# Attention with a gated feed-forward factor: the output projection by Strassen's method, and the row sums of the query projection moved

## The chip, the cores and the metric

The kernel runs on one NeuronCore of a Trainium2 chip, as one program with the engines TensorE (PE, matmuls into PSUM), VectorE (DVE), ScalarE (ACT), GpSimd (POOL) and SyncE (SP, which issues the DMAs here). The metric is the device time of one execution in microseconds. Each engine works through its own instructions in order; semaphores tie the engines together.

## What is computed

`x` has 2048 rows of 512 (BF16). There are 32 heads of width 128 with cached keys and values of 2048 rows each. With `xn = layernorm(x)`:

```python
q = (xn @ wq).reshape(heads)                     # 512 -> 32 x 128
p = softmax(q @ k_cache.T * Dh**-0.5)            # per head, 2048 x 2048
s = concat(p @ v_cache) @ wo                     # 4096 -> 512, the output projection
gate = xn @ W_gate; up = xn @ W_up               # 512 -> 1792
g = silu((relu(gate) * up) @ W_down)             # 1792 -> 512
out = x + s * g
```

## The kernel before

It is written engine by engine with explicit semaphores. It has two stages.

**Feed-forward stage** (`emit_gate_up`, `emit_down`). For each of four quarters `Q` of the rows and each of 14 chunks `fc` of the inner width, four 512-wide matmuls make the gate product, four the up product; ScalarE takes the relu, VectorE multiplies. After the 14 chunks `emit_down` makes `g_sb`. The layer norm (`ln_task`) runs inside the first quarter, and DMA transposes write `xnT`. After the last `emit_down`, VectorE makes four sums and differences of the quarters of `xnT` in `emit_tx` (tensor `TX`, lines 661 to 672); GpSimd makes the like of a pair of heads' query weights (`emit_sw`, tensor `SW`).

**Attention stage.** A block `b` is one head `h = b // 4` and one quarter `Q = b % 4` of the queries; there are 128 blocks. A block has eight pairs `p` of key tiles. For each pair, TensorE makes two score tiles (`emit_S_tile`, L806), ScalarE takes their exponential (L818), and TensorE multiplies them by the values (`emit_PV_tile`, L915, eight matmuls 129 wide, the last column giving the softmax's sum). The score pairs run three pairs ahead (`LAG`) of the value products; the plan below is keyed by the block and pair of the value products. A block's result stays in the one accumulator `ps_acc`. At the block's end VectorE normalizes it (`emit_norm_block`, L835 and L838) into one of eight `Onorm` buffers, and a DMA transpose on SyncE's queue writes it to `OT_store`. The next block's first value product waits for the normalization.

**PSUM slots.** Score pairs share a ring of three slots (`ring_acquire`, two banks each) with all inserted groups of matmuls (`emit_M`). Acquisition is strictly in turn and waits until the slot's last reader is done: for a score pair its exponential, for an inserted group its last VectorE operation.

**Inserted groups.** A plan (`at(b, p, ...)`) puts groups of other matmuls into the blocks, at pair 0 or 4:
- `emit_qp`: the query projection of the first two heads, plainly.
- `emit_st`: the query projection of a later pair of heads by Strassen's method, seven products in four steps (two, two, two, one product) for each half of the columns, so eight steps per pair of heads in eight blocks, at p=0.
- `emit_oproj_tile` (lines 755 to 778): the output projection of a group `g` of four heads, 16 row tiles of four 512-wide matmuls (L761), each added by VectorE into the FP32 sum `s_acc` (L774). One tile per block, at p=4, or behind `emit_st`'s single-product step in the same slot. The groups 0 to 6 go this way.
- For group 6, `emit_base` multiplies `s_acc` by `g_sb` and adds it into `x_sb` (L786, L789), tile by tile.
- `emit_final_tile` (L949): the last group's tiles in the last blocks and after them; VectorE multiplies by `g_sb` (L957), adds to `x_sb` (L973), and a DMA writes the output (L978).

SyncE's queue carries, in the order of the code, the loads of keys, values, `wq` and `wo`, the transposes and the output; an instruction on it that waits holds those behind it.

Of the kernel before, what the change touches and what calls it, by code (L numbers as in the profile page):

```python
# [5 lines left out]
BF16 = mybir.dt.bfloat16  # L6
# [46 lines left out]
def bass_recurrent_scan__mha_block_cached__glu_gated_reglu__prompt_kernel(  # L53
# [18 lines left out]
    NQ = 512  # L72
# [14 lines left out]
    NON = 8  # L87
    NQT = 12
    WSC = 512.0
    assert H % 4 == 0 and QB == 4 and (G * QB) % NON == 0 and NON % QB == 0  # L90
# [19 lines left out]
    with ExitStack() as es:  # L110
# [17 lines left out]
        x_sb = S_([128, NT, D], BF16, "x_sb")  # L128
# [9 lines left out]
        PT = [S_([128, 2, NQ], BF16, "PT") for _ in range(NPB)]  # L138
        es_b = ExitStack()
# [5 lines left out]
        xn_sb = SB_([128, NT, D], BF16, "xn_sb")  # L145
# [28 lines left out]
        sem_T = newsem()  # L174
        sem_out = newsem(16)
# [40 lines left out]
        for b in range(2):  # L216
            tok_pool = sem_pool.sig(pool.memset(V_sb[b][:, :, Dh:VW], 2.0))
# [82 lines left out]
        def t_toks(g):  # L300
            return [(sem_ob[i], 16 * TPB * (g + 1)) for i in range(NON)]

# [178 lines left out]

        gr_free = [None] * NSLOT
# [32 lines left out]
        def emit_gate_up(Q):  # L515
            qs = slice(Q * NQ, (Q + 1) * NQ)
            h_tok = None
            for fc in range(FC):
# [27 lines left out]
                h_tok = finish_gate_up(Q, fc, s, gtok, gu_tok)  # L546
            return h_tok
# [54 lines left out]
        fin_tmp = [S_([128, D], BF16, "fin_tmp") for _ in range(4)]  # L602
        TX = S_([128, 4, DC // 2, S // 2], F16, "TX")
        SW = [S_([128, 4, DC // 2, Dh], F16, "SW") for _ in range(2)]
        cu = S_([128, NQ], F32, "cu")
# [50 lines left out]
        HS = S // 2  # L656
        HC = DC // 2
        tx_tok = []
        sw_tok = {}

        def emit_tx():
            b11 = xnT[:, 0:HC, 0:HS]
            b12 = xnT[:, 0:HC, HS:S]
            b21 = xnT[:, HC:DC, 0:HS]
            b22 = xnT[:, HC:DC, HS:S]
            _wait_all(dve, [t for Q in range(QB) for t in xt_ready[Q]])
            t1 = sem_T.sig(dve.tensor_tensor(TX[:, 0], b12, b11, ALU.subtract))
            sem_T.sig(dve.tensor_tensor(TX[:, 2], b22, b12, ALU.subtract))  # L668
            _wait(dve, t1)
            t2 = sem_T.sig(dve.tensor_tensor(TX[:, 1], b22, TX[:, 0], ALU.subtract))  # L670
            _wait(dve, t2)
            tx_tok.append(sem_T.sig(dve.tensor_tensor(TX[:, 3], TX[:, 1], b21, ALU.subtract)))

# [24 lines left out]
        def emit_st(pr, c, step, *banks):  # L698
# [33 lines left out]
            if step == 1:  # L732
                if c == 0:
                    _wait(pe, sw_tok[(pr, 1)])
                    _wait(pe, tx_tok[0])
# [19 lines left out]
        def emit_oproj_tile(g, n, bank):  # L755
            if n == 0:
                _wait_all(pe, t_toks(g))
                _wait(pe, wo_tok(g))
            ins = None
            for hh in range(G):  # L760
                ins = pe.matmul(ps_r[:, bank, 0:D], OT_store[g % 2][:, hh, n * 128:(n + 1) * 128],  # L761
                                Wo_sb[g % 2][:, hh, :], start=(hh == 0), stop=(hh == G - 1))
            otok = sem_op.sig(ins)
            if n == NT - 1:
                opg_tok[g] = otok
                if g + 2 < NG:
                    _wait(sp, otok)
                    issue_wo(g + 2)
            _wait(dve, otok)
            if g == 0:  # L770
                atok = sem_opa.sig(dve.tensor_copy(s_acc[:, n, :], ps_r[:, bank, 0:D]))
            else:
                atok = sem_opa.sig(
                    dve.tensor_tensor(s_acc[:, n, :], s_acc[:, n, :], ps_r[:, bank, 0:D], ALU.add)  # L774
                )
            if g == NG - 2:
                emit_base(n, atok)
            return atok
# [3 lines left out]
        def emit_base(n, after_tok):  # L782
            _wait(dve, after_tok)
            if n == 0:
                _wait(dve, glu_done_tok)
# [311 lines left out]
```

## Time and profile before

| | us |
|---|---|
| median of 3 runs (1280.49 to 1281.59) | 1280.52 |
| the profiled execution's own time | 1280.7 |
| its span, first to last instruction | 1279.4 |
| TensorE busy | 1257.1 |
| ScalarE busy | 1011.1 |
| VectorE busy | 458.8 |
| GpSimd busy | 97.5 |

The feed-forward stage ends near 157 us; the attention stage fills the rest. Busy times are unions of the recorded instructions. Matmuls are pipelined, so one matmul's recorded duration is longer than the distance to the next; prices of matmuls are therefore taken from starts, or from runs of many. "L12" is line 12 of the kernel whose profile it is. Square brackets at the end of a timeline row give the idle time ahead of the instruction and what ended it.

### The profile page before, as it was taken

What the parts mean: (1) busy time and instruction counts of PE and PEld (TensorE: products, weight loads), DVE (VectorE), ACT (ScalarE), POOL (GpSimd) and SP (SyncE); (2) the same over time, 40 slices, a digit from 0 to 9 for tenths busy, and PEclk for the clock granted to TensorE, in tenths of its full rate; (3) what the DMA queues carried; (4) which work ended last, traced back from release to release, by engine and by line L of the source; (5) the groups of instructions that cost most, each with busy time, mean ns of one, the idle gap of its engine ahead of it and who ended that gap; (6) DMA issues with size and microseconds to landing.
All of it is one profiled execution on the core that took longest, in us unless ns stands there. A gap on an engine that the chain in (4) does not pass through costs nothing.

```text
span 1279.4 us, 26927 instructions
## 1 busy us (share of the span) xinstructions
PE 1257.1 (98%) x11740; PEld 828.7 (65%) x11965; DVE 458.8 (36%) x807; ACT 1011.1 (79%) x1112; POOL 97.5 (8%) x100
## 2 busy tenths in 40 slices
PE   9999989999999999999999999999999999999998
PEld 5444456666666666666666666666666666666665
DVE  7433342222332332333333333333333333335455
ACT  3322369998888888888888888888888888888985
POOL 2200020100001010101010010101010101000000
PEclk9999989999999999999999999999999999999999
DMA  9700002323322232322132332332231222232212
GB/s 268 153 1 1 1 18 51 59 50 59 50 50 55 67 59 47 59 49 57 35 58 47 75 51 46 59 67 55 50 59 34 59 47 54 51 67 47 50 18 75
DMA packets 233588, 72.14 MB, mean 56 GB/s; under 512 B 211200, under 2 KB 233472, under 8 KB 233472
## 3 DMA queue, kind: packets, MB, share of 16 engines
q1 hardware_dynamic: 232800, 70.02, 27.8%
q8 instruction: 95, 1.56, 0.5%
q10 hardware_dynamic: 672, 0.39, 0.1%
q14 instruction: 21, 0.17, 0.0%
HBM read 32.77 MB, written 2.10 MB: 27 GB/s over the span
## 4 chain that ended last, share of the span: by engine, by line
PE 86%; ACT 12%; issue 1%; DVE 1%; DVEq 0%
PE ps_acc L915 33%; PE ps_r L806 27%; ACT PT L818 12%; PE ps_r L761 7%; PE ps_r L717 6%; PE ps_acc L562 4%; PE ps_r L543 4%; PE ps_r L539 4%; PE ps_r L949 1%; PE ps_r L645 1%; PE ps_r L375 0%; DVE fin_tmp L957 0%; PE ps_r L441 0%; DVE TX L670 0%; DVE TX L668 0%
## 5 line engine op out<-in xcount | busy, mean ns | idle before, releaser
L818 ACT ACTIVATE PT<-ps_r 128x1024 bf16<-128x1024 f32 x1024 | 960.9, 1036 | 155.1 <-PE ps_r L806 145.3
L915 PE MATMUL ps_acc<-V_sb,PT 128*128 128x129 bf16 x8192 | 764.3, 220 | 9.9 <-ACT PT L818 0.9
L915 PEld LDWEIGHTS ps_acc<-V_sb,PT 128*128 128x128 bf16 x8192 | 612.8, 98 | 246.0 <-ACT PT L818 19.7
L806 PE MATMUL ps_r<-QT_sb,KT_sb 128*128 128x512 bf16 x1849 | 672.3, 380 | 6.2 <-DVE QT_sb L722 5.2
L806 PEld LDWEIGHTS ps_r<-QT_sb,KT_sb 128*128 128x128 bf16 x2048 | 191.9, 98 | 6.5 <-DVE QT_sb L722 5.4
L835 DVE RECIPROCAL rz_sb<-ps_acc 128x4 f32<-128x4 f32 x127 | 23.2, 183 | 445.7 <-PE ps_acc L915 445.7
L774 DVE TENSOR_TENSOR s_acc<-s_acc,ps_r 128x512 f32<-128x512 f32 x96 | 66.0, 688 | 214.4 <-PE ps_r L761 211.4
L761 PE MATMUL ps_r<-Wo_sb,OT_store 128*128 128x512 bf16 x442 | 114.2, 379 | 0.5
L681 POOL TENSOR_SCALAR Wq_sb<-Wq_sb 128x1024 bf16<-128x1024 bf16 x15 | 41.6, 2771 | 856.7 <-DMA Wq_sb<-in_A_wq_dram 856.7
L838 DVE TENSOR_TENSOR Onorm<-ps_acc,rz_sb 128x512 bf16<-128x512 f32 x127 | 87.8, 692 | 4.4
L761 PEld LDWEIGHTS ps_r<-Wo_sb,OT_store 128*128 128x128 bf16 x448 | 43.8, 98 | 52.9 <-ACT PT L818 1.1
L498 ACT ACTIVATE gr_sb<-ps_r 128x512 bf16<-128x512 f32 x55 | 32.6, 596 | 51.0 <-PE ps_r L539 50.4
L504 DVE TENSOR_TENSOR hT<-gr_sb,ps_r 128x512 bf16<-128x512 bf16 x55 | 37.8, 687 | 46.8 <-PE ps_r L543 41.7
L717 PE MATMUL ps_r<-TX,SW 128*128 128x512 f16 x180 | 48.6, 379 | 0.5
L562 PE MATMUL ps_acc<-Wd_sb,hT 128*128 128x512 bf16 x219 | 48.7, 379 | 0.3
L543 PE MATMUL ps_r<-xnT,Wu_sb 128*128 128x512 bf16 x165 | 42.8, 379 | 0.2
L722 DVE TENSOR_TENSOR QT_sb<-cu,ps_r 128x512 bf16<-128x512 f32 x60 | 41.3, 688 | 4.3
L539 PE MATMUL ps_r<-xnT,Wg_sb 128*128 128x512 bf16 x165 | 42.6, 379 | 0.2
L722 DVE TENSOR_TENSOR cu<-cu,ps_r 128x512 f32<-128x512 f32 x60 | 41.3, 688 | 0.0
L562 PEld LDWEIGHTS ps_acc<-Wd_sb,hT 128*128 128x128 bf16 x224 | 21.9, 98 | 26.4
L722 DVE TENSOR_TENSOR QT_sb<-cv,ps_r 128x512 bf16<-128x512 f32 x60 | 38.3, 681 | 0.0
L717 PEld LDWEIGHTS ps_r<-TX,SW 128*128 128x128 f16 x180 | 17.6, 98 | 21.3 <-ACT PT L818 1.5
(85 smaller groups left out, 419.7 us busy)
## 6 DMA issues: line engine op xcount, KB each, us to landing
V_sb<-in_A_v_cache_dram SPq DMA_DIRECT2D x32, 512.0 KB, 4.2
Wq_sb<-in_A_wq_dram SPq DMA_DIRECT2D x16, 256.0 KB, 2.9
Wo_sb<-in_A_wo_dram SPq DMA_DIRECT2D x8, 512.0 KB, 3.6
OT_store<-Onorm SPq DMA_TRANSPOSE x127, 2.5
Wd_sb<-in_B_W_down_dram SPq DMA_DIRECT2D x1, 1792.0 KB, 14.1
x_sb<-in_A_x_dram SPq DMA_DIRECT2D x3, 512.0 KB, 8.5
out_dram<-x_sb SPq DMA_DIRECT2D x6, 256.0 KB, 2.1
Wg_sb<-in_B_W_gate_dram SPq DMA_DIRECT2D x1, 640.0 KB, 9.7
```

The costliest lines, as they stand in the source:

```text
L539: ins = pe.matmul(g_ps, Wg_sb[:, c, fs], xT[:, c, xs], start=(c == 0), stop=(c == DC - 1))
L543: ins = pe.matmul(u_ps, Wu_sb[:, c, fs], xT[:, c, xs], start=(c == 0), stop=(c == DC - 1))
L562: ins = pe.matmul(ps_acc[:, jb, 0:D], hT[par][:, fc, j * 128:(j + 1) * 128], Wd_sb[:, fc, :], start=(fc == 0), stop=(fc == FC - 1))
L681: k = sem_sw.sig(pool.tensor_scalar(wflat, wflat, WSC, None, op0=ALU.mult))
L717: ins = pe.matmul(ps_r[:, bank, :], L(i), R(i), start=(i == 0), stop=(i == HC - 1))
L722: return sem_qpe.sig(dve.tensor_tensor(dst, a, ps_r[:, bank, :], op))
L761: ins = pe.matmul(ps_r[:, bank, 0:D], OT_store[g % 2][:, hh, n * 128:(n + 1) * 128], Wo_sb[g % 2][:, hh, :], start=(hh == 0), stop=(hh == ...
L774: dve.tensor_tensor(s_acc[:, n, :], s_acc[:, n, :], ps_r[:, bank, 0:D], ALU.add)
L806: ins = pe.matmul(ps_r[:, 2 * s + tt, :], KT_sb[h % 2][:, t * 128:(t + 1) * 128], QT_sb[qt_slot[(h, Q)]][:], start=True, stop=True)
L818: act.activation(PT[pb][:], ps_r[:, 2 * s:2 * s + 2, :], ACTF.Exp, scale=scale if h < 2 else scale / WSC)
L838: dve.tensor_tensor(Onorm[ob][:], o_ap, rz_sb[:].to_broadcast([128, 4, Dh]), ALU.mult))
L915: ins = pe.matmul(o_ap, PT[pb][:, tt, j * 128:(j + 1) * 128], V_sb[vb][:, t, 0:VW], start=(t == 0 and j % 2 == 0), stop=(t == KT - 1 and j ...
```

## The change

**Output projection.** For the groups 0 to 6, `emit_oproj_tile` gives way to `emit_os`. The 2048 x 512 result of a group and its operands are cut into halves: rows (first and second 1024), inner width (two heads and two heads), columns (256 and 256). Seven products of halves, in the order of four steps (1 and 2; 6 and 5; 3 and 7; 4), are made for two row tiles of each half at a time: a product is four matmuls 256 wide in one bank. Their results are added straight into the four quarters of `s_acc`, which now hold running sums over the groups in Strassen's intermediate form. Only after group 6 two more additions per four row tiles turn them into the result. The operands' sums come from `emit_ox` on VectorE (tensor `OX`, FP16, four operations per half of the columns) and `emit_wx` on GpSimd (tensor `WX`, with `Wo` scaled by 1024 in place). The values' sum column is set so that the normalized output is 1024 times larger; the factors are taken out in `emit_base` and in the final tiles.

**Plan.** In blocks 16 to 121 every block has one step of `emit_os` and, up to block 121, one of `emit_st`, at p=0 and p=4 in separate slots; the two-product one comes first. `emit_st` begins two blocks later (block 2), and the plain projection of head 1 moves to p=0 of blocks 0 and 1. Group 6's last six steps lie two to a block in 122 to 124; block 125 has no group. `emit_ox` runs at pairs 2 and 3 of the first and eighth block of a group; `emit_base` at set places in blocks 116 to 125 through a queue.

**Row sums.** `emit_tx` is cut into eight operations of 1024 elements and called in the third quarter of the feed-forward stage.

**Memory.** `x_sb` is given up after the feed-forward stage; `TX` lies in the former `xn_sb`; x comes back tile by tile into `xr_sb` (16 DMAs) for `emit_base`, which now adds into `s_acc` in FP32. The final addition reads `s_acc` and writes `g_sb`, from which the output goes. `Onorm` has four buffers in place of eight.

The core of the diff:

```diff
-    NON = 8
+    NON = 4
...
+        def emit_tx(k):
+            c, i = divmod(k, 4)
+            lo = slice(c * NQ, (c + 1) * NQ)
+            hi = slice(HS + c * NQ, HS + (c + 1) * NQ)
...
+            if i == 0:
+                t = dve.tensor_tensor(X[0], b12, b11, ALU.subtract)
...
+                if Q == QB - 2 and 2 <= fc < 10:
+                    emit_tx(fc - 2)
...
-            for hh in range(G):
-                ins = pe.matmul(ps_r[:, bank, 0:D], OT_store[g % 2][:, hh, n * 128:(n + 1) * 128],
-                                Wo_sb[g % 2][:, hh, :], start=(hh == 0), stop=(hh == G - 1))
...
+        def emit_wx(g):
+            W, X = Wo_sb[g % 2], WX[g % 2]
...
+            k = sem_wx.sig(pool.tensor_scalar(wflat, wflat, WOSC, None, op0=ALU.mult))
...
+            k = sem_wx.sig(pool.tensor_tensor(X[:, 0], b12, b11, ALU.subtract))
+            sem_wx.sig(pool.tensor_tensor(X[:, 2], b22, b12, ALU.subtract))
...
+            k = sem_wx.sig(pool.tensor_tensor(X[:, 1], b22, X[:, 0], ALU.subtract))
...
+        def emit_ox(g, c, i):
...
+            if i == 0:
+                _wait_all(dve, t_toks(g, c))
+                _wait(dve, os_tok.get("x"))
+                ox_tok["k"] = sem_ox.sig(dve.tensor_tensor(OX[:, 0], a21, a22, ALU.add))
...
+        def emit_os(g, q, step, *banks):
...
+            def prod(k, bank):
+                for j in range(2):
...
+                    for i in range(GH):
+                        ins = pe.matmul(ps_r[:, bank, j * DH:(j + 1) * DH], L(i), R(i),
+                                        start=(i == 0 and j == 0), stop=(i == GH - 1 and j == 1))
+                return sem_op.sig(ins)
...
+            def acc(k, bank, op=ALU.add, first=False):
+                _wait(dve, os_tok.get((q, k)))
+                if first:
+                    t = dve.tensor_copy(names[k], view(bank))
+                else:
+                    t = dve.tensor_tensor(names[k], names[k], view(bank), op)
+                os_tok[(q, k)] = sem_opa.sig(t)
...
+            if step == 0:
...
+                p1 = prod(1, banks[0])
+                p2 = prod(2, banks[1])
+                _wait(dve, p1)
+                acc("11", banks[0], first=f)
+                k1 = acc("21", banks[0], first=f)
+                _wait(dve, p2)
+                return [k1, acc("11", banks[1])]
+            if step == 1:
+                _wait(pe, ox_tok[(g, c)])
...
+            p4 = prod(4, banks[0])
...
+            k1 = acc("21", banks[0], ALU.subtract)
+            k2 = acc("22", banks[0])
             if g == NG - 2:
-                emit_base(n, atok)
...
+                t = sem_opa.sig(dve.tensor_tensor(c22, c22, c21, ALU.add))
...
+                t = sem_opa.sig(dve.tensor_tensor(c12, c12, c22, ALU.add))
...
+        def issue_xr(k):
+            n = base_order[k]
+            if k >= 4:
+                _wait(sp, base_done[base_order[k - 4]])
+            sem_xr[k % 4].sig(sp.dma_start(xr_sb[:, k % 4:k % 4 + 1, :], x_t[:, n:n + 1, :]))
...
-                dve.tensor_tensor(x_sb[:, n, :], x_sb[:, n, :], s_acc[:, n, :], ALU.add)
+                dve.tensor_tensor(s_acc[:, n, :], s_acc[:, n, :], xr_sb[:, k % 4, :], ALU.add))
...
-                dve.tensor_tensor(x_sb[:, n, :], x_sb[:, n, :], fin_tmp[fb][:], ALU.add))
+                dve.tensor_tensor(g_sb[:, n, :], s_acc[:, n, :], fin_tmp[fb], ALU.add))
...
-        at(0, 4, (emit_qp, 1, 1, 0), (emit_qp, 1, 1, 1))
-        at(1, 4, (emit_qp, 1, 1, 2), (emit_qp, 1, 1, 3))
+        at(0, 0, (emit_qp, 1, 1, 0), (emit_qp, 1, 1, 1))
+        at(1, 0, (emit_qp, 1, 1, 2), (emit_qp, 1, 1, 3))
...
+                it = (emit_os, 1 if i % 4 == 3 else 2, g, i // 4, i % 4)
+                if g < NG - 2 or i < 10:
+                    osteps[b0 + i] = it
                 else:
+                    at(b0 + 10 + (i - 10) // 2, 4 * (i % 2), it)
+            for c in range(2):
+                for i in range(4):
+                    side.setdefault((b0 + 7 * c, 2 + i // 2), []).append((emit_ox, g, c, i))
...
+            if 0 < pr < NPR:
+                c, step = r // 4, r % 4
+                q = (emit_st, 1 if step == 3 else 2, pr, c, step)
+                first, second = (o, q) if step == 3 and o else (q, o)
+                at(b, 0, first)
+                if second:
+                    at(b, 4, second)
...
+        base_at = [(LB - 8 + k // 2, 2 + k % 2) for k in range(4)]
+        base_at += [(LB - 4 + k // 2, 2 + k % 2) for k in range(4)]
+        base_at += [(LB - 1 + k // 2, 2 + k % 2) for k in range(4)]
+        base_at += [(LB + 1, 1 + k) for k in range(4)]
...
-        _wait(dve, glu_done_tok)
-        emit_tx()
         emit_sw(1)
+        emit_wx(0)
...
+            if pq == 2 and bq % GB == 8 and 0 < bq // GB < NG - 1:
+                emit_wx(bq // GB)
```

More of the change, by code (lines that the diff above doesn't have):

```diff
@@ L174, in bass_recurrent_scan__mha_block_cached__glu_gated_reglu__prompt_kernel @@
         sem_T = newsem()
+        sem_ox = newsem()
+        sem_xr = [newsem(16) for _ in range(4)]
+        sem_wx = newsem()
         sem_out = newsem(16)
@@ L766, in emit_oproj_tile @@
                 if g + 2 < NG:
-                    _wait(sp, otok)
+                    _wait(sp, p4)
                     issue_wo(g + 2)
[L769 to L775, printed above, removed]
-            if g == NG - 2:
-                emit_base(n, atok)
@@ L1046, in bass_recurrent_scan__mha_block_cached__glu_gated_reglu__prompt_kernel @@
                     emit_sw(pr)
+            if pq == 1 and bq == (NG - 1) * GB:
+                for k in range(4):
+                    issue_xr(k)
+            if pq == 2 and bq % GB == 8 and 0 < bq // GB < NG - 1:
+                emit_wx(bq // GB)
             if items:
@@ L1054, in bass_recurrent_scan__mha_block_cached__glu_gated_reglu__prompt_kernel @@
             emit_PV_tile(gq, 1)
-        assert not plan
+        assert not plan and not side and not base_queue
         emit_M([(emit_final_tile, 1, NT - 8), (emit_final_tile, 1, NT - 7)])
```

214 lines of the change are left out of this document (150 added, 64 removed).

## The prediction

> **What bounds the kernel now.** I read the page's busy shares and chain first, then one steady block in the timeline, then the places where TensorE stood still.
>
> ```profile
> span 1279.4 us, 26927 instructions
> ...
> PE 1257.1 (98%) x11740; PEld 828.7 (65%) x11965; DVE 458.8 (36%) x807; ACT 1011.1 (79%) x1112; POOL 97.5 (8%) x100
> ...
> PE 86%; ACT 12%; issue 1%; DVE 1%; DVEq 0%
> ```
>
> TensorE (PE) is busy 98% and holds 86% of the chain. Busy alone proves little, so here is a block (one head, one quarter of the queries, eight pairs of key tiles), from the timeline: start, duration, engine, line.
>
> ```profile
> 728.88 0.59 PE L806 MATMUL ps_r<-QT_sb,KT_sb 128*128 128x512 bf16 x2
> 729.08 0.18 DVE L835 RECIPROCAL rz_sb<-ps_acc 128x4 f32<-128x4 f32 x1 [2.42 <-PE ps_acc L915]
> 729.30 0.69 DVE L838 TENSOR_TENSOR Onorm<-ps_acc,rz_sb 128x512 bf16<-128x512 f32 x1
> 729.31 0.59 PE L717 MATMUL ps_r<-TX,SW 128*128 128x512 f16 x2
> ...
> 730.55 1.28 DVE L722 TENSOR_TENSOR QT_sb<-cv,ps_r 128x512 bf16<-128x512 f32 x2
> ...
> 731.49 3.77 ACT L818 ACTIVATE PT<-ps_r 128x1024 bf16<-128x1024 f32 x4 [0.63 <-PE ps_r L806]
> ...
> 732.40 0.38 PE L806 MATMUL ps_r<-QT_sb,KT_sb 128*128 128x512 bf16 x1
> 732.62 0.39 PE L915 MATMUL ps_acc<-V_sb,PT 128*128 128x129 bf16 x4
> 732.84 0.38 PE L806 MATMUL ps_r<-QT_sb,KT_sb 128*128 128x512 bf16 x1
> ...
> 733.28 0.59 PE L806 MATMUL ps_r<-QT_sb,KT_sb 128*128 128x512 bf16 x2
> 733.72 1.03 PE L761 MATMUL ps_r<-Wo_sb,OT_store 128*128 128x512 bf16 x4
> ...
> 734.78 0.69 DVE L774 TENSOR_TENSOR s_acc<-s_acc,ps_r 128x512 f32<-128x512 f32 x1 [2.95 <-PE ps_r L761]
> ...
> 737.89 0.18 DVE L835 RECIPROCAL rz_sb<-ps_acc 128x4 f32<-128x4 f32 x1 [2.42 <-PE ps_acc L915]
> ```
>
> A score tile and its four value matmuls take 732.84-732.40 = 0.44 us, so a pair takes 0.885 and a block's eight pairs 7.08. This block lasts 737.89-729.08 = 8.81, which is 7.08 plus the two inserted groups of four 512-wide matmuls at 0.863: TensorE has no gap. ScalarE needs at most 0.94 for the exponentials of a pair (3.77 for four) and sat idle 0.63 before these four. A block is therefore TensorE's work, and what is taken from that work shortens it, down to ScalarE's 8 x 0.94 = 7.5 us.
>
> **The matmuls of the output projection.** Removed: 7 groups x 16 tiles x 4 = 448 matmuls 512 wide. Added: 7 groups x 4 (two row tiles of each half) x 7 products x 4 = 784 matmuls 256 wide, each with its own weight load. The chain of waits gives durations of runs of matmuls:
>
> ```profile
> 0.76 4.00 PE ps_r L375 x18
> ...
> 7.47 0.89 PE ps_r L441 x16
> ...
> 342.33 0.86 PE ps_r L761 x4
> ```
>
> 512 wide: 0.863/4 = 0.2158 us, so 96.7 us go. No warm 256-wide matmul exists here. 128 wide, one load each, is 0.89/16 = 0.0556; on the straight line between the two, 256 costs 0.0556 + (0.2158-0.0556)/3 = 0.109, so 85.5 come: **-11.2**. The bounds: half of the 512 price (0.1079, -12.1), and the only 256-wide row, L375 at the program's start, 4.00/18 = 0.222 (+77.3). Two more views decide between them, the windows of a stall that is treated below and the weight loads of L645 (512 wide) just after it. Columns of the windows: window, length, busy of PE, PEld, DVE, ACT, POOL with counts, granted clock.
>
> ```profile
> 160.60:165.78 5.18, 0.00 (x0) 0.00 (x0) 4.99 (x5) 0.86 (x1) 4.19 (x3) 0.73 0.00 0
> 165.78:167.00 1.22, 1.22 (x6) 0.71 (x7) 0.00 (x0) 0.00 (x0) 0.00 (x0) 0.50 0.00 0
> ...
> 169.00:169.50 0.50, 0.50 (x2) 0.15 (x1) 0.00 (x0) 0.50 (x1) 0.00 (x0) 0.50 0.00 0
> ...
> 170.00:171.00 1.00, 1.00 (x9) 0.53 (x8) 0.71 (x2) 0.00 (x0) 0.00 (x0) 1.00 0.00 0
> ```
> ```profile
> 168.33 0.15 PEld L645 LDWEIGHTS ps_r<-xnT,Wq_sb 128*128 128x128 bf16 x1 [0.28 <-issue]
> ...
> 168.76 0.15 PEld L645 LDWEIGHTS ps_r<-xnT,Wq_sb 128*128 128x128 bf16 x1 [0.28 <-issue]
> ```
>
> The clock there is 0.50, and L645 starts every 168.76-168.33 = 0.43 us, twice 0.2158, as 0.222 is about twice 0.109. So I take 0.109 and hold L375 for a row of the slow clock. [...]
>
> **VectorE's share.** The 16 additions per group become 40 (ten per four row tiles: 3, 2, 3 and 2 over the four steps), and eight differences of 1024 elements (`emit_ox`) come in two lots of four. Prices, from the groups by line:
>
> ```profile
> L774 DVE TENSOR_TENSOR s_acc<-s_acc,ps_r 128x512 f32<-128x512 f32 x96 | 66.0, 688 | 214.4 <-PE ps_r L761 211.4 <-remote 0.4
> ...
> L681 POOL TENSOR_SCALAR Wq_sb<-Wq_sb 128x1024 bf16<-128x1024 bf16 x15 | 41.6, 2771 | 856.7 <-DMA Wq_sb<-in_A_wq_dram 856.7
> ...
> L789 DVE TENSOR_TENSOR x_sb<-x_sb,s_acc 128x512 bf16<-128x512 bf16 x16 | 11.1, 692 | 0.5
> ...
> L689 POOL TENSOR_TENSOR SW<-Wq_sb 128x256 f16<-128x256 bf16 x15 | 11.0, 734 | 108.3 <-DVE g_sb L582 107.1
> ...
> L973 DVE TENSOR_TENSOR x_sb<-x_sb,fin_tmp 128x512 bf16<-128x512 bf16 x16 | 6.6, 416 | 0.0
> ...
> L667 DVE TENSOR_TENSOR TX<-xnT 128x2048 f16<-128x2048 bf16 x1 | 1.2, 1224 | 0.0
> ```
>
> Two additions of which the second reads the first's result, from the timeline, start 0.79 apart:
>
> ```profile
> 721.14 0.69 DVE L722 TENSOR_TENSOR cu<-cu,ps_r 128x512 f32<-128x512 f32 x1
> ...
> 721.93 0.69 DVE L722 TENSOR_TENSOR cv<-cu,ps_r 128x512 f32<-128x512 f32 x1
> ```
>
> 7 x 24 x 0.69 = 116 us, plus 56 x 0.69 = 38 (0.69 lies between 416 ns for 512 and 1224 for 2048): VectorE goes from 459 to some 610 us, under half the span. What matters is when a PSUM slot comes free. There are three; each score pair and each inserted group takes the next, so the third pair after a group waits for the group's last VectorE operation. Count from a block's start (728.88 above). The group at p=0 has its three operations behind the normalization and is done at 731.83, 2.95; the third pair after it starts at 732.40, 3.52. The new group at p=4 starts at 4.83; its first product ends at 5.27 and its first addition runs 0.2 later (734.78 against matmuls that end at 734.58), at 5.47; three at a pitch of 0.62 ((730.55-729.30)/2 for operations that don't read each other) end at 7.4, and their slot is wanted at 3.52+4.40 = 7.92. In the blocks with four differences before it (14 of them) VectorE gets free at 2.95+4x0.67 = 5.6, and the three end at 7.5. Both fit: **0**. If each addition waits for the one before, the pitch is 0.79, the 14 late ones end at 7.9 and cost up to 0.1 each, 1.4 in all; a gain is excluded, since no pair waits now.
>
> **GpSimd** scales Wo (2048 elements, two of L681, 5.5 us) and forms four differences of 512 elements (two of L689 each, 5.9 us) once per group (`emit_wx`), eight blocks (some 70 us) ahead of their use; the query weights' work in its queue comes four blocks before and after: 0. Were it late, step 1 of a group would wait.
>
> **Sums over rows (`emit_tx`) moved into the feed-forward stage.** Today they hold VectorE, then TensorE:
>
> ```profile
> 158.29 1.22 DVE L667 TENSOR_TENSOR TX<-xnT 128x2048 f16<-128x2048 bf16 x1
> ...
> 165.04 0.69 DVE L722 TENSOR_TENSOR QT_sb<-cu,ps_r 128x512 bf16<-128x512 f32 x1
> 165.78 0.61 PE L806 MATMUL ps_r<-QT_sb,KT_sb 128*128 128x512 bf16 x1 [5.19 <-DVE QT_sb L722]
> ```
>
> TensorE stands 5.19 us because the first Strassen group's slot is freed only behind the four sums; then it runs at a clock of 0.50 from 165.78 to about 169.7, as the windows show, which loses half of 3.9, 1.95. Both go: **-7.1** (at the least -5.2, if the clock falls anyway). What is late next: that group now comes two blocks later, some 17 us, when sums and weight differences are long done. In the feed-forward stage two groups of four 512-wide matmuls pass per 1.73 us while VectorE needs one 0.69; a half sum of 0.69 fits into the rest: 0.
>
> **The end.** The plan leaves block 125 without a group. Its first value matmul waits for the normalization, which above ends at 729.99, 1.11 after the block's start; with only one score tile (0.22) to do before it, and 0.2 until one engine sees another's end, TensorE stands about **+1.1** (0 to 1.3). The `emit_base` pairs (two operations of 0.69) lie two to a block in blocks 116-124, and in 125; behind a three-operation group they end at 2.95+4x0.69 = 5.7, as the differences do: 0 (at most 0.2 in each of four blocks). x comes back in 16 loads on SyncE's queue, each waiting for an `emit_base` long before the block's transposes: 0. Last, the final addition now reads the FP32 sum, which costs 692 ns (L789's form) instead of 416. The last of them:
>
> ```profile
> 1268.21 0.69 DVE L957 TENSOR_TENSOR fin_tmp<-ps_r,g_sb 128x512 bf16<-128x512 f32 x1 [0.22 <-PE ps_r L949]
> ...
> 1271.29 0.69 DVE L957 TENSOR_TENSOR fin_tmp<-ps_r,g_sb 128x512 bf16<-128x512 f32 x1 [0.23 <-PE ps_r L949]
> ...
> 1276.13 0.68 DVE L957 TENSOR_TENSOR fin_tmp<-ps_r,g_sb 128x512 bf16<-128x512 f32 x1
> 1276.73 0.75 DVE L973 TENSOR_TENSOR x_sb<-x_sb,fin_tmp 128x512 bf16<-128x512 bf16 x2
> ```
>
> From 1268.21 VectorE is close to saturated: nine additions x 0.28 = 2.5, less part of the 0.23: **+2.3** (1.6 to 2.5). Four Onorm buffers instead of eight: a transpose has four blocks, some 35 us: 0.
>
> **Sum.** -11.2 - 7.1 + 1.1 + 2.3 = -14.9 against the profiled execution's own 1280.7: 1265.8. That execution lies 0.2 above the median of 1280.52, so **1265.6**.
>
> **Rivals.** (1) Slots come free late: the gain in the blocks is eaten by score pairs waiting for accumulations. For it: VectorE's work per inserted group doubles or triples. Against it: the 0.4 to 0.5 us of slack. If each of the 112 steps loses 0.07, 7.8 us go: 1273.4. (2) The other side: a 256-wide matmul costs more than its width. It decides where 784 prices reach 96.7+3.7 us (what the other terms bring together), that is at 0.128 us; at L375's 0.222 the time is 1280.5+77.3-3.7 = 1354. Against it: the width-128 row with a load per matmul. [...] (3) The stall at the start isn't removed but paid in the feed-forward stage, because the sums delay the gate product there: 1265.6+7.1 = 1272.7. Against it: 1.04 free of every 1.73.
>
> **How the numbers follow.** A measurement of this kernel tells about 0.2% (2.6 us) from no change. Forecast 0.76, its own range 1262 to 1269 (256-wide between 0.108 and 0.112, the other terms at their bounds). Rival 1 0.12 (0.10 faster, 0.01 within, 0.01 slower), rival 2 0.07 (all slower), rival 3 0.05 (faster). Faster 0.91, same 0.01, slower 0.08; I move 0.02 to the middle for waits nobody listed: 0.89, 0.03, 0.08. The range 1262 to 1273 leaves out rival 2, the worse half of rival 1 and little else.
>
> **What would show it.** In the changed kernel: runs of eight 256-wide matmuls at 0.87 us; blocks of 8.8 us with no wait of L806's successor on VectorE; no idle near 160 us and a granted clock of 1.00 there; one idle of 1.1 us on TensorE near the start of block 125; final additions of 0.69 us. The forecast is wrong if score matmuls wait for `s_acc` operations, if 256-wide runs are longer than 1.0, or if ScalarE shows no idle time between its fours.

## The result and the profile after

The changed kernel takes 1265.95 us (median of 4 runs, 1265.24 to 1265.96) against 1280.51 (1280.43 to 1281.59): a ratio of 0.9883, 95% interval 0.9866 to 0.9900. The forecast was 1265.6. The profiled execution took 1265.24, its span 1263.9.

From the page of the changed kernel, the span, the busy shares and the chain by engine:

```profile
span 1263.9 us, 28351 instructions
...
PE 1255.1 (99%) x12301; PEld 860.1 (68%) x12301; DVE 599.4 (47%) x1043; ACT 1013.9 (80%) x1112; POOL 163.0 (13%) x135
...
PE 97%; ACT 2%; DVE 1%; issue 0%; DMA 0%; DVEq 0%
```

TensorE's share of the chain went from 86% to 97%: nearly nothing else is left on the path. VectorE took 141 us more work (599.4 against 458.8) and GpSimd 66, beside it.

Two blocks from the timeline (start, duration, engine, line; rows between are left out). The second has the operand sums at the start of a group (`emit_ox`, L811 to L819) and a two-product step of the output projection at p=4:

```profile
690.39 0.18 DVE L988 RECIPROCAL rz_sb<-ps_acc 128x4 f32<-128x4 f32 x1 [1.66 <-PE ps_acc L1068]
...
698.57 0.59 PE L959 MATMUL ps_r<-QT_sb,KT_sb 128*128 128x512 bf16 x2
698.77 0.18 DVE L988 RECIPROCAL rz_sb<-ps_acc 128x4 f32<-128x4 f32 x1 [1.82 <-PE ps_acc L1068]
...
701.43 0.68 DVE L811 TENSOR_TENSOR OX<-OT_store 128x1024 f16<-128x1024 bf16 x1
...
703.35 0.69 DVE L819 TENSOR_TENSOR OX<-OT_store,OX 128x1024 f16<-128x1024 bf16 x1
703.40 1.04 PE L842 MATMUL ps_r<-Wo_sb,OT_store 128*128 128x256 bf16 x8
704.04 1.88 DVE L860 TENSOR_TENSOR s_acc<-s_acc,ps_r 128x512 f32<-128x512 f32 x3
...
706.50 0.38 PE L959 MATMUL ps_r<-QT_sb,KT_sb 128*128 128x512 bf16 x1
...
707.58 0.18 DVE L988 RECIPROCAL rz_sb<-ps_acc 128x4 f32<-128x4 f32 x1 [1.66 <-PE ps_acc L1068]
```

The second block lasts 707.58-698.77 = 8.81: 7.08 for the pairs, 0.863 for four matmuls 512 wide, and 0.87 for eight 256 wide, 0.109 each. The block before it, 8.38, has four of them. The three additions end at 704.04+1.88 = 705.92, 7.35 after the block's start at 698.57; the score pair that takes their slot starts at 706.50, at 7.93. They are 0.58 early, even in a block with differences.

The start and the end, as the timeline has them, and the two waits of TensorE for a normalization (columns: who waited, for what, us in total, times, longest):

```profile
157.53 1.89 PE L681 MATMUL ps_r<-xnT,Wq_sb 128*128 128x512 bf16 x8
...
160.56 7.44 ACT L971 ACTIVATE PT<-ps_r 128x1024 bf16<-128x1024 f32 x8 [1.76 <-PE ps_r L959]
```
```profile
157.00:163.00 6.00, 6.00 (x56) 3.80 (x54) 2.05 (x3) 3.95 (x5) 4.07 (x5) 1.00 0.01 3
163.00:169.00 6.00, 6.00 (x59) 3.97 (x58) 2.26 (x4) 5.00 (x6) 5.92 (x3) 1.00 0.11 22
```
```profile
PE ps_acc L1068 <- DVE Onorm L991: 0.9, 1, 0.9
...
PE ps_r L1040 <- ACT Onorm L1016: 0.6, 1, 0.6
```
```profile
1259.69 0.68 DVE L1126 TENSOR_TENSOR g_sb<-s_acc,WX 128x512 bf16<-128x512 f32 x1
1260.29 0.69 DVE L1110 SCALAR_TENSOR_TENSOR WX<-ps_r,g_sb 128x512 bf16<-128x512 f32 x1
1260.89 1.28 DVE L1126 TENSOR_TENSOR g_sb<-s_acc,WX 128x512 bf16<-128x512 f32 x2
```

TensorE is busy all the time from 157 to 169 at a granted clock of 1.00 (the windows, the column behind POOL's). The one bubble inside the blocks is that of block 125. The wait of 0.6 lies in the end, at 1253.59: ScalarE's share of the last block's normalization waits for a reciprocal that stands behind the final additions in VectorE's queue. From 1255.48 on VectorE works without a gap, 0.60 us per operation.

The reciprocals that close the blocks 0, 15, 111 and 126 split the 15.5 us of the span. Before, then after:

```profile
174.09 0.18 DVE L835 RECIPROCAL rz_sb<-ps_acc 128x4 f32<-128x4 f32 x1 [2.42 <-PE ps_acc L915]
...
294.79 0.18 DVE L835 RECIPROCAL rz_sb<-ps_acc 128x4 f32<-128x4 f32 x1 [6.29 <-PE ps_acc L915]
...
1129.01 0.18 DVE L835 RECIPROCAL rz_sb<-ps_acc 128x4 f32<-128x4 f32 x1 [5.96 <-PE ps_acc L915]
...
1259.46 0.18 DVE L835 RECIPROCAL rz_sb<-ps_acc 128x4 f32<-128x4 f32 x1 [2.01 <-PE ps_acc L915]
```
```profile
166.10 0.18 DVE L988 RECIPROCAL rz_sb<-ps_acc 128x4 f32<-128x4 f32 x1 [5.96 <-PE ps_acc L1068]
...
285.99 0.18 DVE L988 RECIPROCAL rz_sb<-ps_acc 128x4 f32<-128x4 f32 x1 [5.60 <-PE ps_acc L1068]
...
1111.55 0.18 DVE L988 RECIPROCAL rz_sb<-ps_acc 128x4 f32<-128x4 f32 x1 [1.82 <-PE ps_acc L1068]
...
1241.80 0.18 DVE L988 RECIPROCAL rz_sb<-ps_acc 128x4 f32<-128x4 f32 x1 [1.48 <-PE ps_acc L1068]
```

| stretch | before | after | difference | of which work that the plan puts into another stretch | the rest |
|---|---|---|---|---|---|
| start to block 0 | 174.09 | 166.10 | -7.99 | -0.86 | -7.13 |
| blocks 1 to 15 | 120.70 | 119.89 | -0.81 | -0.43 | -0.38 |
| blocks 16 to 111 | 834.22 | 825.56 | -8.66 | +0.86 | -9.52 |
| blocks 112 to 126 | 130.45 | 130.25 | -0.20 | +0.43 | -0.63 |
| to the end of the span | 19.94 | 22.10 | +2.16 | 0 | +2.16 |

The column of moved work is a count from the plan, at 0.432 us for two matmuls 512 wide. Two products of the query projection leave the first stretch and one the second, and all three come in the blocks 112 to 126 (+1.30). One output-projection tile (0.863) goes the other way: the kernel before has 95 of its 112 tiles in the blocks 16 to 111, the changed kernel six whole groups, the work of 96.

### The profile page after: what moved, and what is told of

It is laid out like the page before. It is cut to its first block, busy times and chain, and to the rows that moved or that the text cites. A ratio compares the mean times of both kernels' runs of the same rounds, so it can differ in the third digit from the quotient of the medians.

```text
span 1263.9 us, 28351 instructions
## 1 busy us (share of the span) xinstructions
PE 1255.1 (99%) x12301; PEld 860.1 (68%) x12301; DVE 599.4 (47%) x1043; ACT 1013.9 (80%) x1112; POOL 163.0 (13%) x135
## 4 chain that ended last, share of the span: by engine, by line
PE 97%; ACT 2%; DVE 1%; issue 0%; DMA 0%; DVEq 0%
PE ps_acc L1068 36%; PE ps_r L959 34%; PE ps_r L737 7%; PE ps_r L842 7%; PE ps_acc L596 4%; PE ps_r L575 4%; PE ps_r L571 4%; ACT PT L971 2%; PE ps_r L1102 1%; PE ps_r L681 1%; DVE WX L1110 0%; DVE g_sb L1126 0%; DMA x_sb<-in_A_x_dram 0%; PE ps_r L448 0%; DVE stats L326 0%
## 5 line engine op out<-in xcount | busy, mean ns | idle before, releaser
L959 PE MATMUL ps_r<-QT_sb,KT_sb 128*128 128x512 bf16 x2048 | 736.6, 379 | 0.0
L860 DVE TENSOR_TENSOR s_acc<-s_acc,ps_r 128x512 f32<-128x512 f32 x264 | 167.7, 682 | 162.2 <-PE ps_r L842 162.2
L737 PE MATMUL ps_r<-xn_sb,SW 128*128 128x512 f16 x180 | 48.6, 379 | 0.0
L842 PE MATMUL ps_r<-WX,OX 128*128 128x256 f16 x336 | 45.8, 273 | 0.0
L842 PEld LDWEIGHTS ps_r<-WX,OX 128*128 128x128 f16 x336 | 32.9, 98 | 9.8
L790 POOL TENSOR_SCALAR Wo_sb<-Wo_sb 128x2048 bf16<-128x2048 bf16 x7 | 37.6, 5365 | 0.6
```

The costliest lines, as they stand in the source:

```text
L737: ins = pe.matmul(ps_r[:, bank, :], L(i), R(i), start=(i == 0), stop=(i == HC - 1))
L842: ins = pe.matmul(ps_r[:, bank, j * DH:(j + 1) * DH], L(i), R(i), start=(i == 0 and j == 0), stop=(i == GH - 1 and j == 1))
L860: t = dve.tensor_tensor(names[k], names[k], view(bank), op)
L959: ins = pe.matmul(ps_r[:, 2 * s + tt, :], KT_sb[h % 2][:, t * 128:(t + 1) * 128], QT_sb[qt_slot[(h, Q)]][:], start=True, stop=True)
```

## The experiments

Each is the changed kernel with the edit that is shown, except the two that start from the kernel before (said there). "The changed kernel's" time is 1265.95, span 1263.9.

### The row sums

First the move alone, made in the kernel before: `emit_tx` in its eight parts in the feed-forward stage, with `TX` in the former `xn_sb`, and nothing else.

```diff
+                if Q == QB - 2 and 2 <= fc < 10:
+                    emit_tx(fc - 2)
...
-        emit_tx()
```

> The kernel before with one part of the change alone: the eight row sums in the third quarter of the feed-forward stage (TX then lies in the former xn_sb). Output projection, plan, final additions as before. Theory: 5.2 us of standing and 1.95 us of slow clock go, and nothing comes back in the feed-forward stage: 1280.5 - 7.1 = 1273.4 (1272.5 to 1274). Rival (the sums' time is paid in the feed-forward stage instead): 1280.5. Rival (only the standing is regained, the clock falls anyway): 1275.3.

Measured: 1274.99 (1274.58 to 1275.38), ratio 0.9953 (0.9939 to 0.9968), above the range expected. From its timeline, the reciprocals of the blocks 0 and 126, and from its chain of waits the end's wait for the last output transfer:

```profile
167.04 0.18 DVE L847 RECIPROCAL rz_sb<-ps_acc 128x4 f32<-128x4 f32 x1 [2.42 <-PE ps_acc L927]
...
1252.42 0.18 DVE L847 RECIPROCAL rz_sb<-ps_acc 128x4 f32<-128x4 f32 x1 [2.02 <-PE ps_acc L927]
```
```profile
SPq L1079 <- DMA out_dram<-x_sb: 2.5, 1, 2.5
```

Block 0 ends 7.05 earlier than in the kernel before, block 126 7.04 earlier: the -7.1 of the prediction, and not a tenth given back between. That the time moved by only 6.0 (from 1280.96, the kernel before measured beside it) lies behind the work: the last transfer kept the end for 2.5 us in the profiled execution, where it is 1.4 before. The rival by which the feed-forward stage pays for the sums falls: from its first gate matmul to its last down matmul that stage takes 151.11 us here, and 151.11 in the run with halves of 256 below, which has no sums in that stage.

Then the reverse, the changed kernel with all eight sums behind the feed-forward stage:

```diff
-                if Q == QB - 2 and 2 <= fc < 10:
-                    emit_tx(fc - 2)
...
+        _wait(dve, glu_done_tok)
+        for k in range(8):
+            emit_tx(k)
         emit_sw(1)
         emit_wx(0)
```

> The changed kernel with all eight row sums after the feed-forward stage again, in front of the attention stage's first VectorE work; everything else, the plan with its later first Strassen group too, stays. Theory (the sums themselves held TensorE): eight sums of 0.69 keep VectorE busy from about 158.6 to 164.4, the two casts of block 0's inserted group follow until 165.7, and the score pair that wants that group's slot at about 161.5 waits some 4 us; then TensorE runs some 4 us at a granted clock of 0.50. 1266 + 4 + 1.9 = 1272 (1270 to 1273.5). Rival (the later start of the Strassen groups in the plan removed the stall, not the place of the sums): 1266.

Measured: 1276.72 (1275.78 to 1277.56), 4.7 us above the 1272 expected. From its timeline:

```profile
162.43 1.15 DVE L503 TENSOR_TENSOR xn_sb<-xnT 128x1024 f16<-128x1024 bf16 x1
163.12 5.68 POOL L788 TENSOR_SCALAR Wo_sb<-Wo_sb 128x2048 bf16<-128x2048 bf16 x1
163.50 4.12 DVE L505 TENSOR_TENSOR xn_sb<-xnT 128x1024 f16<-128x1024 bf16 x1
167.54 0.68 DVE L508 TENSOR_TENSOR xn_sb<-xnT,xn_sb 128x1024 f16<-128x1024 bf16 x1
...
170.20 0.61 PE L957 MATMUL ps_r<-QT_sb,KT_sb 128*128 128x512 bf16 x1 [8.62 <-DVE QT_sb L686]
```

One sum took 4.12 us in place of 0.68, exactly beside GpSimd's scaling of `Wo`, which the kernel before does not have; TensorE stood 8.62 us. That is a second cause in one experiment. A version with two sums early and six late,

```diff
-                if Q == QB - 2 and 2 <= fc < 10:
+                if Q == QB - 2 and 2 <= fc < 4:
...
+        for k in range(2, 8):
+            emit_tx(k)
```

> The changed kernel with two of the eight row sums in the feed-forward stage and six after it. VectorE is then busy until about 162.8 and with the two casts until 164.2, so TensorE stands about 2.7 us in place of 4. Theory (the clock falls only behind a standing of some 3 to 5 us, as the one of 5.2 before): no window at 0.50, 1266 + 2.7 = 1268.7. Rival (the clock falls behind a standing of 2.7 us too): 1270.6.

ran into the same: 1274.66 (1274.08 to 1275.57), a sum of 4.00 us beside the scaling, TensorE standing 7.29. It tells nothing of the clock, for which it was meant; the limit of some 3 to 5 us in its theory was my estimate from the one stand of 5.19, and no run shows it. So the scaling was taken away from that place (`emit_wx(0)` in block 8, with the other groups' rule), with all sums late:

```diff
-        emit_wx(0)
...
-            if pq == 2 and bq % GB == 8 and 0 < bq // GB < NG - 1:
+            if pq == 2 and bq % GB == 8 and bq // GB < NG - 1:
```

> As the run with all eight row sums after the feed-forward stage, but the first group's weight differences on GpSimd (scaling of 5.4 us and four differences) come in block 8 instead of beside the sums. There a sum beside GpSimd's scaling took 4.12 us and TensorE stood 8.6. Theory (it was GpSimd's scaling that held this one VectorE operation): the sums take some 1.1 us beside GpSimd's four short differences and 0.7 after them, VectorE is done with the casts at about 166.6, TensorE stands 5 us, then 4 to 6 us at a clock of 0.50: 1266 + 5 + 2.5 = 1273.5 (1272.5 to 1274.5). Rival (VectorE's sum was long for another reason): some 1276.7 as there.

Measured: 1273.19 (1272.10 to 1274.09), as expected. The last sums take 0.68 us again and TensorE's row reads

```profile
166.74 0.61 PE L957 MATMUL ps_r<-QT_sb,KT_sb 128*128 128x512 bf16 x1 [5.18 <-DVE QT_sb L686]
```

5.18 of standing. That this is so near to the 5.19 of the kernel before is chance: there the slot of another group was waited for, behind four longer sums. The granted clock is 0.50 from 165.5 to about 172.3; TensorE works 5.6 of that at half speed (a score tile and its four value matmuls take 168.43-167.57 = 0.86 there, in place of 0.44) and loses 2.8: 8.0 in all, and the span is 8.0 longer. So the later Strassen groups of the plan did not remove the stall by themselves; the place of the sums did. Last, four sums early and four late, with the scaling away, to see whether a short stand leaves the clock alone:

```diff
-                if Q == QB - 2 and 2 <= fc < 10:
+                if Q == QB - 2 and 2 <= fc < 6:
...
+        for k in range(4, 8):
+            emit_tx(k)
...
-        emit_wx(0)
...
-            if pq == 2 and bq % GB == 8 and 0 < bq // GB < NG - 1:
+            if pq == 2 and bq % GB == 8 and bq // GB < NG - 1:
```

> Four sums in the feed-forward stage, four after it, GpSimd's first weight differences in block 8. VectorE is done at about 163.8 and TensorE stands 2.2 us. Where the clock fell so far, it fell 2.4 to 3.3 us after TensorE came to stand. Theory (shorter than that, it doesn't fall): 1266 + 2.2 = 1268.2 and no window at 0.50. Rival (it falls behind any standing): 1266 + 2.2 + 2.5 = 1270.7.

Measured: 1269.18 (1269.06 to 1269.19). TensorE stood 2.18 us, until 163.76, and the clock fell all the same; the windows (window, length, busy of PE, PEld, DVE, ACT, POOL, granted clock):

```profile
163.76:164.00 0.24, 0.24 (x2) 0.12 (x3) 0.00 (x0) 0.00 (x0) 0.00 (x0) 1.00 0.00 0
164.00:165.00 1.00, 1.00 (x9) 0.72 (x8) 0.00 (x0) 0.00 (x0) 0.00 (x0) 0.53 0.00 0
...
166.00:167.00 1.00, 1.00 (x9) 0.72 (x8) 0.00 (x0) 0.30 (x2) 0.00 (x0) 0.50 0.00 0
167.00:168.00 1.00, 1.00 (x11) 0.60 (x9) 0.00 (x0) 0.76 (x1) 0.00 (x0) 0.77 0.00 0
```

It fell some 0.3 us after TensorE had resumed and came back at about 167.5. 2.18 + half of 3.4 = 3.9; the span is 4.0 longer. My expectation that so short a stand would leave the clock at 1.00 fell; the rival's price of 2.5 for the slow clock was too high as well, 1.7 was paid.

### The price of a 256-wide matmul

The kernel before, each output-projection tile made as two halves of four 256-wide matmuls, so that nothing but the matmuls' number and width changes:

```diff
-            for hh in range(G):
-                ins = pe.matmul(ps_r[:, bank, 0:D], OT_store[g % 2][:, hh, n * 128:(n + 1) * 128],
-                                Wo_sb[g % 2][:, hh, :], start=(hh == 0), stop=(hh == G - 1))
+            for k in range(2):
+                for hh in range(G):
+                    ins = pe.matmul(ps_r[:, bank, k * 256:(k + 1) * 256],
...
```

> The kernel before with each output projection tile of the groups 0 to 6 made as two halves of 256 columns: eight matmuls 256 wide, each with its own weight load, for four 512 wide. Same sums, same slots, same additions. Theory (a matmul costs its width and 2 to 3 ns): 112 tiles x (8 x 0.109 - 0.863) = +1.0: 1281.5. Rival (narrower matmuls cost more, as the 0.222 of the warm-up row): 112 x (8 x 0.222 - 0.863) = +102: 1383. Anything above 1287 would put the price of one above 0.115.

Measured: 1282.75 (1281.35 to 1283.16, 10 runs), ratio 1.0013 (1.0004 to 1.0023). From the reciprocal of block 0 to that of block 126 the trace is 1.1 us longer over 112 tiles: 0.010 per tile of 0.863, so eight cost 0.873, **0.109** each. (The other 0.7 us lie ahead of block 0, where the program is unchanged.) At L375's 0.222 the time would have been some 100 us longer (896 x 0.222 - 96.7); that is excluded.

### The slots

One, then two further VectorE copies of the product's bank, into a tile that nobody reads, behind the additions of each step that has three: they hold the slot longer and load VectorE more, and do nothing else. The diff is that of one; for two the count is 2.

```diff
+            def extra(bank):
+                toks = []
                for _ in range(1):
...
+                    os_tok["scr"] = sem_opa.sig(dve.tensor_copy(scr[:], ps_r[:, bank, :]))
...
-                return [k1, acc("11", banks[1])]
+                return [k1, acc("11", banks[1])] + extra(banks[1])
...
```

> The changed kernel with one more VectorE operation (a copy of the second bank, 0.69, into a scratch tile that nobody reads) behind the three of steps 0 and 2 of each Strassen output step; the PSUM slot is given back only after it. 56 steps, 39 us more VectorE work, no matmul more. Theory (the slot is wanted 0.48 us after the third operation's end, 7.93 against 7.35 after the block's start plus some 0.1 to see it): the fourth ends at 7.96, TensorE waits 0.1 to 0.2 in each of the 56: 1266 + 8 = 1274 (1271 to 1277). Rival (VectorE at 47% has room, the slots don't matter): 1266.

> As the run with one more operation, with two. Theory: the fifth ends at 8.57, TensorE waits 0.7 to 0.8 in each of the 56 steps: 1266 + 42 = 1308 (1304 to 1311). Rival (VectorE, then at some 53%, has room): 1266.

Measured: 1270.61 (1270.55 to 1270.67) with one, just below the range given, and 1311.12 (1311.09 to 1311.31) with two, just above it. With one, TensorE's waits show no score matmul, but the blocks of a p=4 two-product step go from 8.82 to 8.91 and the others stay at 8.38: 5.3 us of span over 56 steps, 0.095 each. In one such block the copy ends 7.95 after the block's start, and the score matmul that wants the slot starts at 8.02 in place of 7.93. With two the wait has its own row:

```profile
PE ps_r L968 <- DVE scr L869: 36.2, 56, 0.7
```

46.1 us of span, 0.82 per step. The two copies take 1.41 together and one 0.69, so the second adds 0.72, and 0.095+0.72 is what is seen: behind the edge the second copy costs its full pitch. VectorE is 51% busy there. What sets the time is the order of the slots, not VectorE's share, and in the changed kernel it was one operation away.

### GpSimd's differences beside VectorE's

After the 4.12 us above the question was whether the zero for GpSimd holds in general or because of where its work lies. `emit_wx` was made to run exactly beside `emit_ox`, from the normalization of a group's seventh block on:

```diff
-            if pq == 2 and bq % GB == 8 and 0 < bq // GB < NG - 1:
+            if pq == 1 and bq % GB == 7 and 0 < bq // GB < NG - 1:
+                _wait(pool, norm_tok[bq - 1][0])
```

> The changed kernel with GpSimd's weight differences of the groups 1 to 6 (scaling of 5.37, four differences of 1.16) held back until the normalization of the block in which VectorE makes the four operand differences (the eighth of a group), so that the scaling runs beside them. No work added. Theory (a 16-bit VectorE operation waits for GpSimd's scaling to end): in six blocks one of the four differences takes 3 to 4 instead of 0.69, the two additions of the fourth step end some 2 to 3 later, and the score pair that wants their slot waits 1.5 to 3: 1266 + 6 x 2 = 1278 (1273 to 1284). Rival (no such wait): 1266.

Measured: 1271.58 (1271.53 to 1272.47), 5.6 above the changed kernel: the direction as expected, the size below the range. From the timeline of VectorE, and from the waits:

```profile
347.90 0.69 DVE L742 TENSOR_TENSOR cv<-cu,ps_r 128x512 f32<-128x512 f32 x1
348.51 2.92 DVE L811 TENSOR_TENSOR OX<-OT_store 128x1024 f16<-128x1024 bf16 x1
351.35 0.68 DVE L813 TENSOR_TENSOR OX<-OT_store 128x1024 f16<-128x1024 bf16 x1
```
```profile
PE ps_r L959 <- DVE s_acc L860: 5.4, 6, 0.9
```

GpSimd's scaling runs from 347.24 to 352.61 there. The sum over values is held 2.24 us, the addition from PSUM ahead of it, under the same scaling, is not (0.69). Each of the six times one score pair then waits 0.9, and the span is 6.3 longer, 1.05 per group; the other half of the hold went into slack. In the changed kernel the 14 instances of L811 take 681 to 686 ns: the overlap never happens, because `emit_wx` runs right behind the query weights' work in GpSimd's queue, three blocks ahead of where the code issues it (in block 21 and not in block 24 for this group, 331.86 to 341.9), and 6.7 us ahead of the sums at 348.66.

### The end

First the base (`x` plus the earlier groups times the gate), written as BF16 into the front half of `s_acc`'s rows, so that the last addition reads 16-bit operands:

```diff
-                dve.tensor_tensor(s_acc[:, n, :], s_acc[:, n, :], xr_sb[:, k % 4, :], ALU.add))
+                dve.tensor_tensor(base_bf[:, n, 0:D], s_acc[:, n, :], xr_sb[:, k % 4, :], ALU.add))
...
-                dve.tensor_tensor(g_sb[:, n, :], s_acc[:, n, :], fin_tmp[fb], ALU.add))
+                dve.tensor_tensor(g_sb[:, n, :], base_bf[:, n, 0:D], fin_tmp[fb], ALU.add))
```

> The changed kernel with the base (x plus the first seven groups times g) rounded to BF16 when it is formed, into the front half of its FP32 row, as the kernel before held it in BF16. The final additions then read two BF16 tiles. Theory (the end is VectorE's chain of products and additions, which 16 additions at 0.69 in place of 0.42 lengthened by 2.2): the additions fall back to 0.42 and the end to that of the kernel before: 1266 - 2.2 = 1263.8 (1263.2 to 1264.4). Rival (the end hangs on TensorE's last products or on the output's DMAs): 1266.

Measured: 1263.06 (1262.94 to 1263.30), ratio 0.9859 (0.9844 to 0.9874); span 1261.6. The last operations of its timeline:

```profile
1258.37 0.69 DVE L1111 SCALAR_TENSOR_TENSOR WX<-ps_r,g_sb 128x512 bf16<-128x512 f32 x1
1258.97 0.75 DVE L1127 TENSOR_TENSOR g_sb<-s_acc,WX 128x512 bf16<-128x512 bf16 x2
```

The pair costs 0.94 in place of 1.20. From the reciprocal of block 126 to the end it is 19.93, as in the kernel before (19.94), in place of 22.10: the FP32 addition's term, 2.2, taken back whole. (The span is 2.3 shorter; 0.1 lies ahead of block 0.) Then the plan's empty block filled, by moving group 6's last step from block 124 to 125 (and the base operations there to pairs 2 and 3 of the blocks 125 and 126):

```diff
-                    at(b0 + 10 + (i - 10) // 2, 4 * (i % 2), it)
+                    at(*[(122, 0), (122, 4), (123, 0), (123, 4), (124, 0), (125, 0)][i - 10], it)
...
-        base_at += [(LB + 1, 1 + k) for k in range(4)]
+        base_at += [(LB + 1 + k // 2, 2 + k % 2) for k in range(4)]
```

> The changed kernel with group 6's last step (one product) at the start of block 125 instead of the middle of block 124, and the last four base tiles at pairs 2 and 3 of blocks 125 and 126. Theory (TensorE stands 0.9 at the start of block 125 for want of a group, and the step covers 0.44 and a second score tile 0.22 of it): 1266 - 0.6 = 1265.4 (1265.0 to 1265.8). Rival (blocks with so little inserted work are held by ScalarE at some 7.9 anyway): 1266.

Measured: 1264.56 (1264.41 to 1264.84), ratio 0.9871 (0.9856 to 0.9885). No row of TensorE's waits names VectorE's normalization any more. From block 0 to block 126 the trace is 0.66 shorter, as expected, and not the 0.9 of the row; the rest of the span's 0.8 lies ahead of block 0, where the program is unchanged. Block 125, with a single-product step, now takes 7.90, 0.39 more than its matmuls (see "What was off"). Both edits together:

> Base in BF16 and block 125 filled, together. Theory: the two gains add: 1266 - 2.2 - 0.6 = 1263.2 (1262.6 to 1263.9). Rival for each as in the single runs: 1263.8 or 1265.4 where one of them gives nothing.

Measured: 1262.36 (1262.29 to 1262.62), ratio 0.9854 (0.9837 to 0.9870), span 1261.0: the fastest of all, 3.6 us below the changed kernel. The two gains add: 2.2 behind block 126 and 0.65 ahead of it. By the medians they are 2.9 and 1.4, together 3.6, and all three medians lie below the ranges expected, by 0.1 to 0.4. In three of the four runs of the changed kernel 2.0 to 2.3 us lie outside the span, in these three kernels about 1.3, so stretches of the trace are the better measure of such edits.

## Why the prediction was right

**Matmuls, -11.2.** Confirmed in price and place. 0.109 was read from the 128- and the 512-wide rows; the steady blocks and the halves in the kernel before both give 0.109. In the blocks 16 to 111 lies the work of 96 of the 112 tiles, which by the prediction's prices is -9.6; measured, with the moved tile set right, -9.52. The other 16 (-1.6) share their stretch with the bubble. That L375's 0.222 is not the price at full clock is shown; that it was a row of the slow clock is not shown directly, since the trace's record of the clock begins behind it, at 5.94 us. It rests on the ratio of about two.

**The stall at the start, -7.1.** Confirmed: 7.05 with the move alone, and 7.13 in the first stretch here (7.48 of it within block 0, less 0.35 by which the first score pair behind the feed-forward stage starts later, 157.09 against 156.74; in the run with halves of 256, whose program is that of the kernel before up to there, it starts at 157.18, so the change is not the cause). Both parts are real: the sums late again cost 5.18 of standing and 2.8 of slow clock. The lower bound of -5.2 (the clock falls anyway) didn't come.

**Slots, 0.** The count gave 7.4 to 7.5 against 7.92; measured 7.35, with the differences, against 7.93. The added copies place the edge where the count does: the first costs 0.095, the second 0.72 more. Rival 1, 0.07 lost per step, was one operation away. One reading was wrong without harm: of the 14 blocks with differences only the seven that begin a group have three additions behind them; the other seven have two.

**GpSimd, 0.** Right in size, in part by luck, for its reason was incomplete. The prediction named time ("eight blocks (some 70 us) ahead of their use") and not what VectorE does meanwhile; in three runs a sum of 16-bit operands from SBUF that started under the scaling was held for 2.2 to 3.4 us (2.92 to 4.12 in place of 0.68). The zero holds because the order in GpSimd's queue happens to put the scaling 6.7 us ahead of the sums. This risk was in none of the rivals, though the trace before shows it, at the stall itself:

```profile
159.43 1.69 DVE L668 TENSOR_TENSOR TX<-xnT 128x2048 f16<-128x2048 bf16 x1
161.04 1.68 DVE L670 TENSOR_TENSOR TX<-xnT,TX 128x2048 f16<-128x2048 bf16 x1
```
```profile
160.00 1.64 POOL L690 TENSOR_TENSOR SW<-Wq_sb 128x256 f16<-128x256 bf16 x1
161.61 1.64 POOL L692 TENSOR_TENSOR SW<-SW,Wq_sb 128x256 f16<-128x256 f16 x1
```

Three of the four row sums took 1.57 to 1.69 where the first took 1.22, beside GpSimd differences of 1.53 to 1.64 that take 0.67 elsewhere. The 734 ns by which the prediction prices L689 are a mean of fourteen at 0.67 and this one at 1.63; a group's mean can hide such a row. (In `emit_wx`, where it prices four differences at two of L689 each, 5.9 us, they took 4.6.)

**The end.** The bubble of block 125, +1.1: measured 0.9 as a wait, and 1.0 as what its stretch lacks of the -1.6 (-0.63). The final additions, +2.3: measured 2.16, and 2.2 taken back by the BF16 base. The base operations, the loads of x and the four buffers: no wait of TensorE names them.

**What was off.** ScalarE's floor of 7.5 us per block. Blocks that hold only a single-product step need 7.08+0.43 = 7.51 and take 7.90; a row in such a block names the exponential, and TensorE's value matmul waits for it:

```profile
199.79 0.61 PE L1068 MATMUL ps_acc<-V_sb,PT 128*128 128x129 bf16 x8 [0.23 <-ACT PT L971]
```

The changed kernel has one such block fewer up to block 15 than the kernel before, and that is the -0.38 in the table. The work in a block could be lowered by less than I said before ScalarE sets the time. Of the blocks that the change alters only block 125 came so low: 8.12 for 7.08 of matmuls with its bubble, and 7.90 in the run that fills it. The normalization ends close by, so how the 0.39 divides between the two is open.

**Sum.** By stretches -7.1 (start), -0.4 (floor), -9.5 and -1.6 (matmuls), +1.0 (bubble), +2.2 (end): -15.4, rounded, of the span's -15.5. The forecast had -14.9; the 0.4 of the floor and the 0.2 by which the starts and ends differ from their terms are what it lacked. By the medians the gain is 14.6 and not 15.5, since three of the four runs of the changed kernel spend 2.0 to 2.3 us outside the span, where the profiled run before spends 1.3. That the median comes within 0.4 of the forecast is therefore in part luck; the terms agree on their own.

## What to carry to other kernels

Where TensorE is without gaps, a change of its work can be priced from its own rows by width, if rows of the slow clock are told apart from rows of the fast one first (L645, 512 wide, starts every 0.43 us at a clock of 0.50 in the kernel before; at 1.00 the price is 0.2158). What the side work costs is then a question of dates, not of shares: count when a slot comes free and when its next user is due, in the block where most operations queue ahead. And note for each GpSimd operation which VectorE operations can run beside it: here the sums took 2.92 to 4.12 in place of 0.68 under the scaling, and the scaling 5.68 in place of 5.37 where a sum was running as it began. A plan that keeps such a pair apart by chance should keep it apart on purpose.

## What the runs showed of the hardware that was not expected

**VectorE held by GpSimd.** A 16-bit tensor-tensor operation of 1024 elements, 0.68 us alone, took 4.12, 4.00 and 2.92 when it started under GpSimd's scaling of 2048 elements (5.37 alone, 5.68 when a sum was running as it began), and ended 1.2 us ahead of the scaling's recorded end (167.62 of 168.80; 351.43 of 352.61). In the runs with late sums it took 1.04 to 1.16 when it started beside GpSimd's tensor-tensor operations of 256 elements, and those 0.99 to 1.12 in place of 0.67. Additions with one operand in PSUM kept 0.69 under the scaling. What holds the sums, and why they end 1.2 us ahead of the scaling, was not shown.

**The clock after a short stand.** Stands of five lengths led to a clock of 0.50: 2.18 us (it fell 2.5 after TensorE stopped, when TensorE was at work again), 5.18 (3.9 after), 5.19 (2.4 after, in the kernel before), 7.29 (3.1 after) and 8.62 (3.2 after). The slow stretch lasted 3.4 us behind the first, 6.8 behind those of 5.18 and 5.19, and 10.2 behind the last two: once, twice and three times 3.4. The stand of 0.9 at block 125 left the clock at 1.00. What sets the moment of the fall and the length of the slow stretch was not shown. In these runs the stand of 2.18 cost another 1.7 for the clock and that of 5.18 another 2.8; where between 0.9 and 2.18 a stand ceases to be free was not tried.
